# Attention and expert layer on one core: the order of issue planned anew with SyncE's time per DMA, token-place tables made later, nine head pairs transposed on TensorE

## The chip, the core and the metric

The kernel runs on one core of one Trainium2 chip. The metric is device time in microseconds; before the change the median of three runs is 273.97 us.

## What is computed

There are 4 batches, 8 heads, 768 positions and a head dimension of 64. Attention is local and global with a distance bias, in float32 accuracy:

```
scores = q @ k.T / sqrt(64) - slope[h] * dist
keep   = (key < 8) | (0 <= query - key < 96)
a      = softmax(where(keep, scores, -1e9))
x[b]   = concat over heads of a @ v                        # 768 x 512
```

Then, for each batch, the 128 tokens with the highest `x @ w_gate` go through `relu(xe @ w1) @ w2` (512 to 1024 to 512), weighted by a sigmoid of that score and added to their rows.

## The kernel before, in words

**Pairs and fronts.** Two heads make a pair, so there are 16 pairs (`i`, four for each batch) of 6 query tiles (`t`, 128 queries). For a tile, `attend` makes scores on TensorE (L808, read from the transposed `kT` and `qT`), adds the bias and takes the row maximum on VectorE (L824, out `sn`, `nm`), and takes the exponential on ScalarE (L830, out `pr`). The scores of one tile are called a front here. Then the probabilities are transposed and cut into a float16 high and low part. In an `f` tile TensorE transposes (L858, out `pt`), ScalarE writes the high part `ph` and VectorE the low part `pl` (L357, L358). In a `d` tile ScalarE and VectorE cut first (`pn`, L838 and L845) and a transposing DMA from SyncE's queue (L847) writes `pT`. `blend` multiplies with `vs` and `va` into `po` (L886).

**Preparing a pair.** `prep_pair` cuts q and k into float16 high and low parts and transposes them. For a pair below `PEP` TensorE transposes first (L729) and ScalarE and VectorE cut from PSUM (L737, L739). For the others the strings `KM` and `QM` say which engine cuts: the last two letters of a mode name the engine of the high part and of the low part, P for GpSimd (L710, L720), D for VectorE (L714), A for ScalarE; in a three-letter mode the first letter scales the source in place. Then a transposing DMA brings `k16` to `kT` (L762) and `q16` to `qT` (L767). `k16` and `q16` have one buffer each, the loaded `kn`, `qn` and `vn` two. `VM` says the same for v, which needs no transpose but two small copies `va` (L771, L775).

**Setup.** GpSimd makes index patterns (`setup_iotas`), VectorE the mask and the bias of heads 0 and 1 (L602 to L619), GpSimd the bias of the other heads (L623, L625). `setup_moe` makes the tables with which the expert layer finds tokens: `tie`, `places`, `token` and some small ones, on GpSimd (L275 and L630 to L634).

**Expert layer.** `moe_rank` and `moe_chunk` rank the tokens of a finished batch, gather 128 rows and run three products of split float32 operands for each weight (L428, L450). Its pieces are spread over the fronts of the next batch; the last batch's run alone at the end.

**What sets the order.** All this is entered as steps of a `Program`. A step has an engine, a planned duration, what it reads and writes, and a rank. `Program.order` plays the program through: of the steps of an engine that could start within `WINDOW` ns of the earliest one, the one of lowest rank goes next. It knows a TensorE at half speed after little work, and a port that VectorE and GpSimd share (`port=True`). A DMA step holds the planned SyncE for 60 ns. The result is one list; every engine's queue and SyncE's gets its instructions in that order and runs them in order, waiting only for real data and free buffers. `gates[n]` is front n: a step with a gate can't be planned ahead of it. A gate, a rank or a planned duration moves instructions in the queues and puts no wait on the chip. `LG` and `LGE` gate the loads of pairs, `WLG` those of weights, `PACE`, `AUXG` and `MOEP` the expert layer. `ORD0` is the first pair that uses the order `_D1`, which has one `d` tile (t = 4); the pairs before it and the last use `_BASE`, which has none.

```
if name == "SP":
    e["free"] = start + 60
    dma_free = max(dma_free, start + self.DMA_START) + s["dur"]
    end = dma_free + self.DMA_END
```

Of the kernel before, what the change touches and what calls it, by code (L numbers as in the profile page):

```python
# [18 lines left out]
P = 128  # L19
# [3 lines left out]
GMAX = 8  # L23
LBACK = 96
# [19 lines left out]
_D3 = "d4 f0 b0 d1 d5 f2 b2 b1 f3 b4 b5 b3"  # L44

LG = (-13.9, 0.7)
LGE = {1: (-1, 0.4), 2: (0, 0.7)}
PACE = (9.7, 2.7)
PACE2 = (16.83, 1.13)
AUXG = (2, 300, 6)  # L50
AUXG2 = (2.59, 650.35, 4.4)
MOEP = (1.41, 5.1, 16.8, 42.86)
WLR = (33.6, 0.5)
WLG = (6, 0.5)
BG = 1
BG0 = 1
ORD0 = 10
ORDS = [_BASE] + [_D1]
VR = 0
NR = 6  # L60
FR = 1
VR0 = 5
PEP = 8
TLS = 3
WIN_ = 5.94016
VM = 'PD,PD,PD,PD,PD,PD,PPP,APP,APP,PPP,PPP,PPP,DPP,PPP,PPP,PPP'.split(',')
KM = 'PD,PD,PPP,AD,AD,PD,PD,PD,APP,PD,PD,PD,APP,PD,DPP,APP'.split(',')
QM = 'APP,PPP,PD,PD,PD,PD,PD,PD,PD,PD,PD,APP,APP,PD,DPP,AD'.split(',')

# [27 lines left out]
class Program:  # L97
# [14 lines left out]
    def __init__(self):  # L112
        self.steps = []

    def add(self, eng, dur, fn, w=(), r=(), rank=0.0, tail=0, cols=None, port=False):
# [11 lines left out]
        self.steps.append(dict(eng=eng, dur=dur, fn=fn, deps=deps, rank=rank, tail=tail, bufs=bufs,  # L127
                               heavy=cols is not None, port=port or eng == "POOL",
                               cols=dur * 1.9 if cols is None else cols))

    TICK, FULL = 10240 / 3, 3060
# [15 lines left out]
    def order(self):  # L147
# [20 lines left out]
        port = {"DVE": 0.0, "POOL": 0.0}  # L168
        while len(issued) < len(steps):
            best = None  # L170
            for name, e in engines.items():
                pick = None
                for k in e["ready"]:
                    start = max(ready_t[k], e["free"])
# [14 lines left out]
            start, k, name = best  # L189
# [4 lines left out]
                    taken.add(b)  # L194
                    slots[b.ring].remove(min(slots[b.ring]))
            if name == "SP":
                e["free"] = start + 60
                dma_free = max(dma_free, start + self.DMA_START) + s["dur"]
                end = dma_free + self.DMA_END
            else:  # L200
                dur = s["dur"]
                if name == "PE" and self.filler:
                    while start - e["free"] >= self.FILL_MIN:
                        d = self.pe_time(ticks, e["free"], 213, 512)
                        if e["free"] + d > start + self.FILL_OVER:
# [35 lines left out]
def kernel(  # L241
# [15 lines left out]
    NT = S // P  # L257
# [7 lines left out]
    DE = 2 * D + 2  # L265
# [216 lines left out]
    with ExitStack() as fast:  # L482
# [156 lines left out]
        def setup_tie():  # L639
# [4 lines left out]
        a0 = add(-20)  # L644
        a0("SP", 50, lambda: nc.sync.dma_start(
            out=par_i.rearrange("p a w -> p (a w)"), in_=ints.bitcast(I32).partition_broadcast(P)), w=[B_par_i])
        a0("POOL", 1900, setup_iotas, w=[B_set])
        a0("DVE", 70, setup_par, w=[B_par], r=[B_par_i])
        flags_at = len(prog.steps)
        add(40)("DVE", 490, setup_flags, w=[B_flag], r=[B_par])  # L650
        a0("DVE", 700, setup_causal, w=[B_set])
        a0("DVE", 1500, setup_tables, w=[B_set], r=[B_par])
        bias_steps = {}
        for h in range(H):
            bias_steps[h] = len(prog.steps)
            if h in BHD:
                add(6 * (h // 2) - 7)("DVE", 440, lambda h=h: bias_head(h), w=[(B_bias, h)], r=[B_set])
            else:
                add(6 * (h // 2) - 7)("POOL", 1470, lambda h=h: bias_head_pool(h), w=[(B_bias, h)], r=[B_set])
        add(4)("POOL", 1490, setup_moe, w=[B_pos, B_tie, B_pl, B_scol, B_tok, B_filled])  # L660
        add(4)("DVE", 100, setup_tie, w=[B_tie], r=[B_pos])
        add(4)("SP", 300, lambda: nc.sync.dma_start(out=wg_bc, in_=w_gate.partition_broadcast(P)), w=[B_wg])

        def load_weights():
            n = 0
            for src, hi, lo, bh, bl, cols in ((w1, w1_hi, w1_lo, B_w1h, B_w1l, F), (w2, w2_hi, w2_lo, B_w2h, B_w2l, DM)):
                for c in range(src.shape[0] // P):
                    for o in range(0, cols, F32_ROW):
                        sl = slice(o, o + F32_ROW)
# [3 lines left out]
                        a("SP", 730, lambda raw=raw, src=src, c=c, sl=sl: nc.sync.dma_start(  # L673
                            out=raw(), in_=src[c * P:(c + 1) * P, sl]), w=[raw])
# [15 lines left out]
        def prep_pair(i):  # L690
# [103 lines left out]
        def attend(i, t, n, by_dma):  # L794
# [39 lines left out]
            if by_dma:  # L834
# [6 lines left out]
                else:  # L841
# [89 lines left out]
        def finish(a, b, x, t0):  # L931
# [46 lines left out]
        for i in range(NP):  # L978
# [23 lines left out]
            if hp == NPAIR - 1:  # L1002
# [214 lines left out]
```

## Time and profile before

| | us |
|---|---|
| runs, median (lowest, highest) | 273.97 (273.80, 277.82) |
| profiled execution | 275.46 |
| its span, first to last instruction | 273.5 |
| TensorE, VectorE, ScalarE, GpSimd busy | 234.9, 201.6, 204.0, 175.6 |
| mean granted clock of TensorE | 0.917 |

The profiled execution is one run: its own time is 0.5% above the median, and 1.96 us of it lie outside its span. A busy engine is one that has an instruction in it, also one that is held up in it or runs at half clock. No engine is busy all the time, so what sets the end has to be looked for stretch by stretch.

### The profile page before, as it was taken

Reading aid. Unit: us, or ns where it says so; the run is one execution under the profiler, and the core shown is the slowest. Engines: PE = TensorE matmul, PEld = TensorE weight load, DVE = VectorE, ACT = ScalarE, POOL = GpSimd, SP = SyncE. Lnnn points to the kernel's source line nnn. Section 1 sums busy time; section 2 is a strip of 40 time slices with the busy share of each in tenths; the row PEclk is TensorE's granted clock in tenths of the full one; section 3 lists DMA queues with packets and bytes.
Section 4 is the critical chain, followed back from the end, with each engine's and each line's share of the span. In section 5 each row is a group of like instructions: output and inputs, shape, how many; then the busy total and the mean of one; then the engine's idle time right before and its main releaser. Section 6 shows DMA issues by size and latency. Waiting matters only on the chain.

```text
span 273.5 us, 8161 instructions
## 1 busy us (share of the span) xinstructions
PE 234.9 (86%) x2983; PEld 183.1 (67%) x2983; DVE 201.6 (74%) x735; ACT 204.0 (75%) x521; POOL 175.6 (64%) x211
## 2 busy tenths in 40 slices
PE   7598997979888895884999998998978999989990
PEld 3376786867776673763887685766756878767770
DVE  7869999999797788367776689977559688674120
ACT  2348995979889999785799999996799997180200
POOL 9692295997899948869965764899869360111011
PEclk9659997999999999576599999996599999999999
DMA  4999895888999261999978899999933610511011
GB/s 111 234 196 248 198 223 150 214 220 255 311 232 202 62 148 41 167 289 234 225 169 159 143 177 185 202 290 265 153 90 106 131 41 30 203 41 40 2 43 47
DMA packets 114994, 44.28 MB, mean 162 GB/s; under 512 B 107008, under 2 KB 107648, under 8 KB 114944
## 3 DMA queue, kind: packets, MB, share of 16 engines
q1 hardware_dynamic: 114304, 41.57, 70.1%
q0 software_dynamic: 640, 2.10, 2.3%
q8 instruction: 25, 0.41, 0.6%
q14 instruction: 25, 0.20, 0.2%
HBM read 24.38 MB, written 7.34 MB: 116 GB/s over the span
## 4 chain that ended last, share of the span: by engine, by line
PE 41%; DVE 20%; ACT 19%; DMA 8%; issue 5%; POOL 4%; SPq 1%; POOLq 0%; DVEq 0%; ACTq 0%
PE pt L858 7%; PE po L886 6%; PE ps L808 6%; ACT pr L830 5%; DVE pl L358 5%; PE pm L450 5%; PE pm L428 5%; DMA kn<-in_k_dram 5%; DVE sn L824 5%; ACT ph L357 4%; ACT sg L333 3%; PE pm L323 2%; DMA pT<-pn 2%; PE ps L450 2%; PE ps L428 2%
## 5 line engine op out<-in xcount | busy, mean ns | idle before, releaser
L830 ACT ACTIVATE pr<-sn,nm 128x232 f32<-128x232 f32 (+1 forms) x192 | 83.7, 476 | 7.2 <-DVE nm L824 5.8
L824 DVE CUSTOM_DVE_ANT_0 sn<-ps,bias 128x232 f32<-128x232 f32 (+1 forms) x192 | 66.3, 372 | 13.6 <-PE ps L808 11.7
L358 DVE TENSOR_TENSOR pl<-pt,ph 128x512 f16<-128x512 f32 (+1 forms) x91 | 56.9, 635 | 13.7 <-ACT ph L357 13.1
L858 PE MATMUL pt<-ident,pr 128*128 128x128 f32 x332 | 61.0, 310 | 1.3 <-ACT pr L830 1.2
L808 PE MATMUL ps<-kT,qT 64*128 64x128 f16 (+1 forms) x1056 | 50.9, 225 | 8.8 <-DVE nm L824 3.9
L357 ACT CAST ph<-pt 128x512 f16<-128x512 f32 (+1 forms) x91 | 48.7, 545 | 10.3 <-PE pt L858 9.6
L808 PEld LDWEIGHTS <-qT 64*128 64x128 f16 x1056 | 33.4, 99 | 24.2 <-issue 20.6
L858 PEld LDWEIGHTS pt<-ident,pr 128*128 128x128 f32 x332 | 39.6, 154 | 8.3 <-ACT pr L830 4.3
L886 PEld LDWEIGHTS <-ph 128*128 128x128 f16 (+1 forms) x664 | 36.6, 102 | 10.4 <-issue 2.8
L886 PE MATMUL po<-vs,ph 128*128 128x65 f16 x364 | 42.5, 200 | 0.7 <-ACT num L900 0.6
L909 POOL TENSOR_TENSOR x<-num,dens 128x384 f32<-128x384 f32 x30 | 25.4, 845 | 23.0 <-DVE dens L904 12.3
L886 PE MATMUL po<-va,pl 104*128 104x65 f16 x150 | 30.1, 201 | 11.5 <-DVE pl L358 11.2
L886 PE MATMUL po<-va,ph 104*128 104x65 f16 x300 | 37.1, 200 | 1.4 <-ACT ph L357 0.9
L886 PE MATMUL po<-vs,pl 128*128 128x65 f16 x182 | 34.8, 200 | 0.9 <-DVE pl L358 0.9
L886 PEld LDWEIGHTS <-pl 104*128 104x128 f16 (+1 forms) x332 | 23.4, 102 | 14.6 <-DVE pl L358 14.4
L947 POOL TENSOR_TENSOR xw<-x,wg_bc 128x512 f32<-128x512 f32 x18 | 23.4, 1326 | 0.2
L683 POOL TENSOR_TENSOR w_lo<-xw,w_hi 128x512 fp32r<-128x512 f32 x16 | 20.4, 1275 | 0.5
L333 ACT ACTIVATE sg<-sbc,neg 128x768 bf16<-128x768 f32 x21 | 19.6, 935 | 0.1
L710 POOL TENSOR_SCALAR vs<-vn 128x768 f16<-128x768 f32 x16 | 13.5, 846 | 9.6 <-PE po L886 5.6
L456 POOL DMA_INDIRECT out_dram<-xe,idx x4 | 4.1, 1031 | 21.0 <-DVE xe L454 19.8
L720 POOL TENSOR_TENSOR vs<-vn,vs 128x768 f16<-128x768 f32 x10 | 16.2, 1619 | 1.8 <-DVE vn L710 1.6
L900 ACT COPY num<-po 128x390 f32<-128x390 f32 x30 | 14.5, 484 | 3.0 <-PE po L886 2.7
(189 smaller groups left out, 484.2 us busy)
## 6 DMA issues: line engine op xcount, KB each, us to landing
vn<-in_v_dram SPq DMA_DIRECT2D x32, 192.0 KB, 4.4
out_dram<-x SPq DMA_DIRECT2D x24, 256.0 KB, 4.3
kn<-in_k_dram SPq DMA_DIRECT2D x30, 192.0 KB, 4.1
qn<-in_q_dram SPq DMA_DIRECT2D x30, 192.0 KB, 3.8
xw<-in_moe_w_dram SPq DMA_DIRECT2D x16, 256.0 KB, 4.2
va<-vs SPq DMA_DIRECT2D x16, 243.8 KB, 3.7
va<-vs SPq DMA_DIRECT2D x16, 20.3 KB
kn<-in_k_dram SPq DMA_DIRECT2D x2, 128.0 KB
```

Of the source, the lines that this page charges most:

```text
L333: nc.scalar.activation(sg(), flat(), AF.Sign, bias=neg()[:, t:t + 1], accum_out=rank()[:, t:t + 1])
L357: add("ACT", 50 + int(0.836 * cols), lambda: nc.scalar.copy(hi[1](), ps[1]()), w=[(hi[0], part)], r=[ps[0]])
L358: add("DVE", 40 + int(1.04 * cols), lambda: nc.vector.tensor_tensor(out=lo[1](), in0=ps[1](), in1=hi[1](), op=ALU.subtract), w=[(lo[0], pa ...
L428: nc.tensor.matmul(psh(), lhsT=a()[:, d, :], rhs=w[:, d, sl], start=(j == 0), stop=(j == len(mms) - 1))
L683: a("POOL", 1225, lambda raw=raw, hi=hi, lo=lo, c=c, sl=sl: nc.gpsimd.tensor_tensor(out=lo[:, c, sl], in0=raw(), in1=hi[:, c, sl], op=ALU. ...
L808: nc.tensor.matmul(ps[hh]()[:, at:at + n], lhsT=qT()[rows, l, t, :], rhs=kf[rows, r, o:o + n], start=(j == 0), stop=(j == 2))
L824: nc.vector.tensor_tensor_reduce(out=sn()[:, hh, 0:w], in0=ps[hh]()[:, 0:w], in1=bt, scale=-SCALE / QS, scalar=BIG, op0=ALU.add, op1=ALU.m ...
L830: a("ACT", 209 + int(0.836 * w), lambda hh=hh: nc.scalar.activation(pr()[:, hh, 0:w], sn()[:, hh, 0:w], AF.Exp, bias=nm()[:, hh:hh + 1], s ...
L858: nc.tensor.transpose(pt()[:, blk, hh, :], pr()[:, hh, blk * P:(blk + 1) * P], ident)
L886: nc.tensor.matmul(po()[:, g, cols], lhsT=l, rhs=r, start=(m == 0), stop=(m == len(mms) - 1))
L909: a("POOL", 800, lambda: nc.gpsimd.tensor_tensor(out=xv(), in0=num()[:, :, 1:1 + P].rearrange("p t (h d) -> p t h d", h=2), in1=rb(), op=A ...
L947: a("POOL", 1225, lambda t=t, xw=xw: nc.gpsimd.tensor_tensor(out=xw(), in0=x()[:, t - t0, :], in1=wg_bc, op=ALU.mult), w=[xw], r=[x, B_wg] ...
```

## The change

`Program.add` takes `issue`, the time for which a DMA step holds the planned SyncE: 500 ns, or what a line names. `setup_moe` becomes a step of 4700 ns, gated to front 6, the first of pair 1. Pair 8 goes to TensorE's transposes (`PEP` 9). The order with one `d` tile starts at pair 6 (`ORD0` 6), which gives nine `d` tiles (pairs 6 to 14) for five (10 to 14). Planned durations of setup steps, gates, paces and the engines' modes of some pairs get other values.

```
-LGE = {1: (-1, 0.4), 2: (0, 0.7)}
-PACE = (9.7, 2.7)
-PACE2 = (16.83, 1.13)
-AUXG = (2, 300, 6)
-AUXG2 = (2.59, 650.35, 4.4)
-MOEP = (1.41, 5.1, 16.8, 42.86)
+LGE = {1: (-2.5, 0.4), 2: (-1, 0.7)}
+PACE = (10.25, 2.7)
+PACE2 = (15.74, 1.13)
+AUXG = (1.43, 300, 6.37)
+AUXG2 = (3.2, 1143.26, 5.74)
+MOEP = (1.41, 5.07, 17.14, 42.98)
-WLG = (6, 0.5)
-BG = 1
+WLG = (6, 0.3)
+BG = 3
-ORD0 = 10
+ORD0 = 6
-VR = 0
+VR = 1
-VR0 = 5
-PEP = 8
+VR0 = 4
+PEP = 9
-WIN_ = 5.94016
-VM = 'PD,PD,PD,PD,PD,PD,PPP,APP,APP,PPP,PPP,PPP,DPP,PPP,PPP,PPP'.split(',')
-KM = 'PD,PD,PPP,AD,AD,PD,PD,PD,APP,PD,PD,PD,APP,PD,DPP,APP'.split(',')
-QM = 'APP,PPP,PD,PD,PD,PD,PD,PD,PD,PD,PD,APP,APP,PD,DPP,AD'.split(',')
+WIN_ = 22.2261
+VM = 'PD,APP,PD,PD,PD,PD,PPP,PD,PPP,PPP,PPP,DD,DPP,PPP,PPP,PPP'.split(',')
+KM = 'PD,PD,PPP,PD,DPP,PD,PD,PD,APP,PD,PPP,PD,APP,PD,PD,PD'.split(',')
+QM = 'AD,PPP,PD,PD,PD,PPP,PD,DD,PD,PD,PD,APP,PPP,AD,PPP,DPP'.split(',')
+SUM = 6
...
             if name == "SP":
-                e["free"] = start + 60
+                e["free"] = start + s["issue"]
...
-        a0("POOL", 1900, setup_iotas, w=[B_set])
+        a0("POOL", 2000, setup_iotas, w=[B_set])
...
-        a0("DVE", 700, setup_causal, w=[B_set])
-        a0("DVE", 1500, setup_tables, w=[B_set], r=[B_par])
+        a0("DVE", 900, setup_causal, w=[B_set], port=True)
+        a0("DVE", 1700, setup_tables, w=[B_set], r=[B_par], port=True)
...
-        add(4)("POOL", 1490, setup_moe, w=[B_pos, B_tie, B_pl, B_scol, B_tok, B_filled])
+        moe_at = len(prog.steps)
+        add(4)("POOL", 4700, setup_moe, w=[B_pos, B_tie, B_pl, B_scol, B_tok, B_filled])
...
+        prog.steps[moe_at]["deps"].add(gates[SUM])
```

The heads 0 and 1's bias steps get `port=True` as well. The named issue times are 430 ns for weights and outputs, 2500 for `kT`, 1500 for `qT`, 570 and 780 for the two `va`, 1250 for `pT`.

## Rows read from the trace of the kernel before

**Rows 1.** The page, 40 slices of the span: TensorE's granted clock in tenths.
```profile
PEclk9659997999999999576599999996599999999999
```

**Rows 2.** Stretches, us: length, busy us (instructions) of PE, PEld, DVE, ACT, POOL, clock, DMA share, GB/s.
```profile
7.50:10.70 3.20, 0.06 (x4) 0.01 (x1) 3.13 (x11) 0.03 (x1) 1.43 (x2) 0.80 1.10 240
10.70:20.00 9.30, 8.98 (x68) 6.69 (x67) 6.28 (x21) 5.08 (x12) 8.53 (x12) 0.52 1.00 215
24.00:32.00 8.00, 6.93 (x127) 5.60 (x126) 7.71 (x28) 6.67 (x18) 0.39 (x2) 1.00 1.07 232
80.00:96.00 16.00, 13.30 (x223) 10.46 (x217) 12.60 (x51) 15.51 (x43) 16.00 (x16) 1.00 0.70 148
106.00:110.00 4.00, 1.17 (x16) 0.81 (x15) 4.00 (x7) 4.00 (x10) 4.00 (x3) 0.80 0.15 44
114.00:118.00 4.00, 2.20 (x36) 1.67 (x35) 0.83 (x6) 3.31 (x9) 4.00 (x4) 0.85 1.19 267
122.00:126.00 4.00, 1.26 (x23) 1.14 (x22) 2.26 (x3) 0.72 (x2) 3.05 (x3) 0.93 1.21 174
126.00:136.00 10.00, 9.22 (x112) 7.43 (x113) 7.57 (x34) 8.01 (x22) 9.58 (x10) 0.51 1.04 255
184.00:188.00 4.00, 2.30 (x36) 2.18 (x36) 3.30 (x11) 2.13 (x7) 4.00 (x7) 0.86 1.19 274
188.00:197.00 9.00, 9.00 (x70) 7.20 (x68) 5.64 (x22) 7.86 (x23) 7.47 (x7) 0.50 1.05 205
```

**Rows 3.** Timeline of GpSimd, 2 to 10 us: start us, us, instruction, count.
```profile
2.61 0.21 POOL L596 MEMSET vs<- 128x12 f16 x1
...
4.01 2.56 POOL L275 IOTA places<- 128x768 f16 x1
```

**Rows 4.** Timeline of VectorE, 2 to 13 us, same columns, idle time before in brackets.
```profile
2.07 2.20 DVE L602 TENSOR_SCALAR causal<-rel 128x352 f32<-128x352 f32 x1 [0.67 <-POOL rel L275]
4.19 2.54 DVE L604 TENSOR_SCALAR keep<-rel 128x128 f32<-128x128 f32 x1
...
8.32 0.35 DVE L614 TENSOR_SCALAR keep<-keep 128x360 f32<-128x360 f32 x1
...
10.22 0.41 DVE L739 SCALAR_TENSOR_TENSOR kT<-pm,kT 128x256 f16<-128x256 f32 x1
...
12.06 0.28 DVE L824 CUSTOM_DVE_ANT_0 sn<-ps,bias 128x128 f32<-128x128 f32 x1
```

**Rows 5.** Timeline of VectorE, 106 to 127 us: pair 7's last front, pair 8's first, a q part.
```profile
106.29 0.40 DVE L824 CUSTOM_DVE_ANT_0 sn<-ps,bias 128x232 f32<-128x232 f32 x1
...
116.70 0.29 DVE L824 CUSTOM_DVE_ANT_0 sn<-ps,bias 128x128 f32<-128x128 f32 x1 [2.68 <-PE ps L808]
...
123.74 1.57 DVE L714 SCALAR_TENSOR_TENSOR q<-qn,q 128x768 f16<-128x768 f32 x1 [2.26 <-POOL q L710]
```

**Rows 6.** Timeline of SyncE's queue, 111 to 181 us: start us, us of issue, DMA, count.
```profile
111.36 2.98 SPq L762 DMA_TRANSPOSE kT<-k  x1
...
118.58 0.95 SPq L555 DMA_DIRECT2D qn<-in_q_dram  x1
...
180.66 1.34 SPq L847 DMA_TRANSPOSE pT<-pn  x1
```

**Rows 7.** DMA issues by line: count, median us from issue to landing.
```profile
kT<-k SPq DMA_TRANSPOSE x8, 6.0
```

**Rows 8.** Groups by line: operation and shapes, count, busy us, mean ns, idle us before.
```profile
L729 PE MATMUL pm<-ident,qn 128*128 128x128 f32 x48 | 9.0, 300 | 1.1 <-DVE kT L739 1.1
L858 PE MATMUL pt<-ident,pr 128*128 128x128 f32 x332 | 61.0, 310 | 1.3 <-ACT pr L830 1.2
L358 DVE TENSOR_TENSOR pl<-pt,ph 128x512 f16<-128x512 f32 (+1 forms) x91 | 56.9, 635 | 13.7 <-ACT ph L357 13.1
L845 DVE TENSOR_TENSOR pn<-pr,pn 128x464 f16<-128x464 f32 x5 | 5.3, 1052 | 0.0
```

**Rows 9.** Waits, all of the span: us in total, times, longest.
```profile
PEld L886 <- DMA pT<-pn: 1.7, 2, 1.4
```

More of the change, by code (lines that the diff above doesn't have):

```diff
@@ L46 @@
 LG = (-13.9, 0.7)
-LGE = {1: (-1, 0.4), 2: (0, 0.7)}
-PACE = (9.7, 2.7)
-PACE2 = (16.83, 1.13)
-AUXG = (2, 300, 6)
-AUXG2 = (2.59, 650.35, 4.4)
-MOEP = (1.41, 5.1, 16.8, 42.86)
+LGE = {1: (-2.5, 0.4), 2: (-1, 0.7)}
[4 more added lines that the diff above has]
+MOEP = (1.41, 5.07, 17.14, 42.98)
 WLR = (33.6, 0.5)
-WLG = (6, 0.5)
-BG = 1
+WLG = (6, 0.3)
+BG = 3
 BG0 = 1
-ORD0 = 10
+ORD0 = 6
 ORDS = [_BASE] + [_D1]
-VR = 0
+VR = 1
 NR = 6
 FR = 1
-VR0 = 5
-PEP = 8
+VR0 = 4
+PEP = 9
 TLS = 3
-WIN_ = 5.94016
-VM = 'PD,PD,PD,PD,PD,PD,PPP,APP,APP,PPP,PPP,PPP,DPP,PPP,PPP,PPP'.split(',')
-KM = 'PD,PD,PPP,AD,AD,PD,PD,PD,APP,PD,PD,PD,APP,PD,DPP,APP'.split(',')
-QM = 'APP,PPP,PD,PD,PD,PD,PD,PD,PD,PD,PD,APP,APP,PD,DPP,AD'.split(',')
+WIN_ = 22.2261
+VM = 'PD,APP,PD,PD,PD,PD,PPP,PD,PPP,PPP,PPP,DD,DPP,PPP,PPP,PPP'.split(',')
+KM = 'PD,PD,PPP,PD,DPP,PD,PD,PD,APP,PD,PPP,PD,APP,PD,PD,PD'.split(',')
+QM = 'AD,PPP,PD,PD,PD,PPP,PD,DD,PD,PD,PD,APP,PPP,AD,PPP,DPP'.split(',')
+SUM = 6
 class Buf:
@@ L113, in __init__, with add @@
         self.steps = []
-    def add(self, eng, dur, fn, w=(), r=(), rank=0.0, tail=0, cols=None, port=False):
+    def add(self, eng, dur, fn, w=(), r=(), rank=0.0, tail=0, cols=None, port=False, issue=500):
         k = len(self.steps)
@@ L127, in add @@
         self.steps.append(dict(eng=eng, dur=dur, fn=fn, deps=deps, rank=rank, tail=tail, bufs=bufs,
-                               heavy=cols is not None, port=port or eng == "POOL",
+                               heavy=cols is not None, port=port or eng == "POOL", issue=issue,
                                cols=dur * 1.9 if cols is None else cols))
@@ L490, in add @@
         def add(rank):
-            return lambda eng, dur, fn, w=(), r=(), tail=0, drank=0.0, cols=None, port=False: prog.add(
-                eng, dur, fn, w, r, rank + drank, tail, cols, port)
+            return lambda eng, dur, fn, w=(), r=(), tail=0, drank=0.0, cols=None, port=False, issue=500: prog.add(
+                eng, dur, fn, w, r, rank + drank, tail, cols, port, issue)
         def ring(pool, shape, dtype, name, bufs, free=False):
@@ L656 @@
             if h in BHD:
-                add(6 * (h // 2) - 7)("DVE", 440, lambda h=h: bias_head(h), w=[(B_bias, h)], r=[B_set])
+                add(6 * (h // 2) - 7)("DVE", 440, lambda h=h: bias_head(h), w=[(B_bias, h)], r=[B_set], port=True)
             else:
                 add(6 * (h // 2) - 7)("POOL", 1470, lambda h=h: bias_head_pool(h), w=[(B_bias, h)], r=[B_set])
-        add(4)("POOL", 1490, setup_moe, w=[B_pos, B_tie, B_pl, B_scol, B_tok, B_filled])
+        moe_at = len(prog.steps)
+        add(4)("POOL", 4700, setup_moe, w=[B_pos, B_tie, B_pl, B_scol, B_tok, B_filled])
         add(4)("DVE", 100, setup_tie, w=[B_tie], r=[B_pos])
@@ L673, in load_weights @@
                         a("SP", 730, lambda raw=raw, src=src, c=c, sl=sl: nc.sync.dma_start(
-                            out=raw(), in_=src[c * P:(c + 1) * P, sl]), w=[raw])
+                            out=raw(), in_=src[c * P:(c + 1) * P, sl]), w=[raw], issue=430)
                         aux_gate.append((len(prog.steps) - 1, max(0, WLG[0] + WLG[1] * n)))
@@ L763, in prep_pair @@
                 out=kT().rearrange("p s t c -> p (s t) c")[:, :, 0:P], in_=k16().rearrange("p s t d -> p (s t d)")),
-                w=[(kT, "m")], r=[k16])
+                w=[(kT, "m")], r=[k16], issue=2500)
               firsts()
@@ L768, in prep_pair @@
                 out=qT().rearrange("p s t c -> p (s t) c"), in_=q16().rearrange("p s t d -> p (s t d)")),
-                w=[qT], r=[q16])
+                w=[qT], r=[q16], issue=1500)
             parts(vn, lambda s: vs()[:, :, s, 1:1 + P], vs, VM[i % len(VM)], VR if i else VR0)
@@ L772, in prep_pair @@
                 out=va()[0:LBACK].rearrange("p t s d -> p (t s d)"),
-                in_=vs()[P - LBACK:P, 0:NT - 1].rearrange("p t s d -> p (t s d)")), w=[(va, 0)], r=[vs])
+                in_=vs()[P - LBACK:P, 0:NT - 1].rearrange("p t s d -> p (t s d)")), w=[(va, 0)], r=[vs], issue=570)
             gv = "p t s d -> p t (s d)"
@@ L776, in prep_pair @@
                 out=va()[LBACK:BLK_A].rearrange(gv),
-                in_=vs()[0:GMAX, 0:1].rearrange(gv).to_broadcast([GMAX, NT - 1, 2 * DE])), w=[(va, 1)], r=[vs])
+                in_=vs()[0:GMAX, 0:1].rearrange(gv).to_broadcast([GMAX, NT - 1, 2 * DE])), w=[(va, 1)], r=[vs], issue=780)
             ps = pm()
@@ L848, in attend @@
                     out=pT().rearrange("p s h a t -> p (s h a) t"), in_=pn().rearrange("p s h c -> p (s h c)")),
-                    w=[pT], r=[pn])
+                    w=[pT], r=[pn], issue=1250)
                 left = lambda s, hh, blk: pT()[0:BLK_A if blk else P, s, hh, blk, :]
@@ L937, in finish @@
                 a("SP", 730, lambda t=t: nc.sync.dma_start(out=out[b][t * P:(t + 1) * P, :], in_=x()[:, t - t0, :]),
-                  w=[(B_out[b], t)], r=[x])
+                  w=[(B_out[b], t)], r=[x], issue=430)
                 if b == B - 1:
```

## The prediction, made blind

> **What bounds the kernel now.** I read the page first, for the clock. TensorE is granted less than full speed in a few slices only [rows 1], so there are distinct places where it starved. I then cut the span there [rows 2]; what to see is how little TensorE did, and what clock it got afterwards. From 7.5 to 10.7 us it worked 0.06 us, and in the 9.3 us that follow it has a clock of 0.52, which is the lower level (1.2 of 2.4 GHz), and is busy for 8.98. Around 106, 114 and 122 it worked 1.17, 2.20 and 1.26 us of 4 each, and then 9.22 of 10 at 0.51. Around 184 it worked 2.30 of 4, then 9.00 of 9 at 0.50. Each gap thus costs its idle time, and after it about 10 us at half clock.
>
> The first gap is VectorE's. Its two mask instructions last 2.20 and 2.54 us, where one of such a shape takes 0.35 later [rows 4]. The second ends within 0.2 us of GpSimd's `places` pattern, which runs from 4.01 to 6.57 [rows 3]. So VectorE was held up there while GpSimd had its long instruction.
>
> The gaps at 106 and 114 are pair 8's. Pair 7's last front is read at 106.29, pair 8's first at 116.70, after a wait for the scores [rows 5]. They needed `kT`, whose transposing DMA was issued at 111.36 and takes 2.98 us of SyncE to issue [rows 6] and 6.0 to land [rows 7]. Pair 8 is the first that goes by DMA, and GpSimd, which cuts its k, is full from 80 to 96 (16.00 of 16) [rows 2]. The gap at 122 comes from SyncE's order: a q load issued at 118.58 [rows 6] has to land, GpSimd has to cut it, and VectorE stands 2.26 us before the low part of it [rows 5], with low parts and fronts of the running pair queued behind.
>
> **The change, part by part**, against the profiled execution's 275.46 us; I carry the sum over to the median, 1.49 us lower, unchanged.
>
> *Tables out of the setup.* GpSimd is then done with its small patterns and memsets at 2.82 [rows 3]. Held until there at most, the two mask instructions end at 2.82 + 2 x 0.35 = 3.5 in place of 6.73 [rows 4], and the first low part of `kT` comes at 7.0 in place of 10.22. TensorE's gap there is 3.1, so **-3.1** (0, if the first loads then come late, to -3.1).
>
> *The clock behind it.* Without the gap the clock need not fall at 9.4. At most half of the 8.98 busy us would go (-4.5), at least nothing. VectorE is busy 6.28 of the same 9.3 [rows 2], so much of it is paced elsewhere: **-1.5**, a third.
>
> *The tables made later.* They are planned no earlier than front 6, where GpSimd is empty (0.39 busy of 8 from 24 to 32), so GpSimd pays nothing; if that cover is gone they push pair preparation back by their length, which the plan puts at 4.7 us. But VectorE is full there (7.71 of 8). It can be held up as in the setup, by at most 2.20 + 2.54 - 2 x 0.35 = 4.0, at least by nothing: **+1.0**, nearer to nothing, because its work there is mostly subtractions and fronts and not the kind held in rows 4. The Trainium skill (SBUF — State Buffer, SBUF: two separate sides) says that the port pair of VectorE and GpSimd is locked for a whole instruction, and that a VectorE instruction with two SBUF inputs contends only with GpSimd work that reads SBUF. Patterns and memsets read none, so by that this term would be 0 and the sum 1.0 lower; rows 3 and 4 agree for the mask instructions, and no row shows the other kind.
>
> *Pair 8 on TensorE.* 12 transposes of 0.300 us come to TensorE, +3.6 [rows 8]. From GpSimd go two high parts and one subtraction, from SyncE two transposing DMAs. The wait for pair 8's `kT` goes, and its `kn` and `qn` buffers come free sooner, so pair 10's loads can be issued sooner. The three gaps hold 2.83 + 1.80 + 2.74 = 7.4 us of idle TensorE. What is late next is pair 9, now the first by DMA, out of the same full GpSimd. I keep half: **-3.7** (0 to -7.4). The clock behind, from 126: at most half of 9.22, **-1.9** (0 to -4.6).
>
> *Four more `d` tiles* (pairs 6 to 9). TensorE loses 4 x 4 x 0.310 = -5.0 [rows 8]. With pair 8's transposes its work is **-1.4** (+3.6 if only pair 8's addition is on the path, -5.0 if only the saving is). VectorE pays 4 x (1.052 - 0.635) = 1.7 more [rows 8], hidden while TensorE or ScalarE sets the pace; uncovered, it is those 1.7. SyncE issues four `pT` of 1.34 each [rows 6], 5.4, and loses pair 8's two transposes, some 4 to 6 at `kT`'s price. Behind a `pT` that waits for its `pn` stand the next loads, and behind a late `pT` stands `blend` on TensorE. Of the five before, TensorE's weight loads waited twice for a `pT`, 1.4 us at the longest [rows 9]; the costly one is that of 180.66 [rows 6], ahead of the gap at 184. It cost 1.7 idle and at most 4.5 more by the clock. At one in five, four more bring 0.8 of one; at 2.5 each, nearer to what was surely lost, **+2.0** (0 to 4 x 6.2 = 25, the end of the slower rival).
>
> *SyncE's planned time, gates, paces and modes.* These only move instructions in queues. Counted by letters, beside pair 8, GpSimd loses one subtraction and VectorE gets one, of 1.57 us by the one in rows 5, among 15 pairs: **0** (±1.6). What the new SyncE order is worth at the gap of 122 is in the -3.7 already.
>
> Sum: -3.1 - 1.5 + 1.0 - 3.7 - 1.9 - 1.4 + 2.0 = -8.6. That is 266.9 for the profiled execution and **265.4 us** for the median.
>
> **The rivals.**
>
> *The hole only moves.* Pair 9 starves as pair 8 did, or another order of SyncE frees no wait. For it: GpSimd's full stretch of rows 2 stays. Against it: pair 9 loses the wait for the single `k16` and `q16` that pair 8 held. Then the two middle terms are 0: -8.6 + 5.6 = -3.0, **271.0**. The Trainium skill (DMA: Bandwidth & Descriptors, Issuing engines are not separate DMA queues) calls the time to initiate a DMA usually small relative to the DMA itself, by which planning with it would move little and this rival would be the case. Here 2.98 us of issue stand against 6.0 to landing [rows 6, 7], so the trace speaks against the rule for transposing DMAs.
>
> *Slower: `pT` comes late.* Nine transposing `pT` in SyncE's single queue, the new ones at 80 to 130 us where it also loads, stores and transposes. If two more of them land after their `blend` is due, at 6.2 each, SyncE's backlog has eaten the middle gain too: -3.1 - 1.5 + 1.0 - 1.4 + 12.4 = +7.4, **281.4**. With one it is +1.2, so it decides from the second. Against it: the five before made TensorE wait twice, and only once for long [rows 9].
>
> *All of it comes.* Every gap and its slow clock go, the tables cost nothing: -3.1 - 4.5 - 7.4 - 4.6 - 1.4 + 2.0 = -19, **255**.
>
> **How the numbers follow.** The forecast gets 0.50, the moved hole 0.30, late `pT` 0.12, all of it 0.08. The predicted time is the first, 265.4. Its own range, from the ends of the terms that can't all fall together, is 259 to 270. The range to hold 8 in 10 adds the moved hole with 4 us for the tables' upper end and leaves out most of the last two cases: 258 to 275.5. Two per cent, about what a measurement of this kernel can tell from no change, is 268.5 and 279.5. Faster: nearly all of the forecast, the last case and a little of the moved hole, 0.57. Within: 0.32. Slower: 0.11.
>
> **What would show it.** Setup: the mask instructions under 0.9 us each, the first front read near 9 us, and the clock of the second slice full. If they stay near 2 us, or the first front stays at 12, the first two terms are wrong. Tables: VectorE instructions of over 1.5 us beside `places` after pair 1's first front would show the +1.0 or more. Middle: pair 8's first front within 2 us of pair 7's last; if the same 10 us stand before pair 9's, it is the moved hole. `pT`: waits of TensorE in `blend` for the DMA of `pT`, and how many. The prediction is wrong as a whole if the gaps of TensorE come at other pairs and last as long as before, which rows of this trace can't show beforehand.

## The result, and the profile after

| | before | after |
|---|---|---|
| median, us (lowest to highest, runs) | 273.88 (270.2 to 277.82, 4) | **259.0** (255.73 to 263.38, 4) |
| profiled execution; its span | 275.46; 273.5 | 258.79; 256.7 |
| TensorE, VectorE, ScalarE, GpSimd busy | 234.9, 201.6, 204.0, 175.6 | 224.9, 200.0, 201.4, 175.0 |
| mean granted clock | 0.917 | 0.971 |

The change makes the kernel 14.9 us faster: 0.946 of the time before, interval 0.930 to 0.962. Forecast were 8.6, so the time lies 6.4 us below the predicted 265.4.

Look at the clock first, as before. The page's 40 slices of the kernel after:

```profile
PEclk9997999999999999979979999999979999999999
```

Against [rows 1], nothing under 0.7 is left. The mean clock gives the size: at half clock for a share s of the span the mean is 1 - s/2, so 2 x 0.083 x 273.5 = 45 us before and 2 x 0.029 x 256.7 = 15 us after. TensorE's busy time falls by 10.0 us, though only 1.4 of work were to go.

Stretches of the kernel after, columns as in [rows 2] (101 to 105 is where pair 8 starts now):

```profile
7.50:10.70 3.20, 1.72 (x24) 1.09 (x23) 2.43 (x9) 2.35 (x7) 2.20 (x4) 1.00 1.26 228
10.70:20.00 9.30, 7.30 (x104) 5.48 (x104) 7.75 (x34) 8.06 (x21) 8.70 (x13) 1.00 1.05 216
80.00:96.00 16.00, 14.69 (x241) 11.98 (x239) 14.78 (x56) 15.95 (x42) 16.00 (x15) 1.00 0.73 154
101.00:105.00 4.00, 3.38 (x48) 2.79 (x49) 3.34 (x15) 4.00 (x12) 3.97 (x6) 1.00 1.54 172
126.00:136.00 10.00, 8.81 (x66) 6.34 (x67) 8.50 (x23) 7.83 (x19) 5.45 (x4) 0.83 0.99 219
184.00:188.00 4.00, 2.42 (x42) 1.92 (x40) 3.30 (x11) 4.00 (x14) 3.57 (x5) 0.92 1.00 190
188.00:197.00 9.00, 9.00 (x83) 6.59 (x82) 6.09 (x22) 7.99 (x24) 8.15 (x8) 0.85 0.73 114
```

At the start TensorE works 1.72 us where it worked 0.06, and the 9.3 us behind have the full clock: 104 matmuls in 7.30 busy us, where 68 took 8.98. From 80 to 96 GpSimd is as full as before. At 184 the gap is still there (2.42 of 4), but the clock behind it is 0.85, not 0.50.

VectorE's timeline, the instructions of [rows 4] and [rows 5] (start, us, instruction):

```profile
2.08 0.95 DVE L604 TENSOR_SCALAR causal<-rel 128x352 f32<-128x352 f32 x1 [0.68 <-POOL rel L277]
2.95 0.21 DVE L606 TENSOR_SCALAR keep<-rel 128x128 f32<-128x128 f32 x1
...
7.84 0.42 DVE L742 SCALAR_TENSOR_TENSOR kT<-pm,kT 128x256 f16<-128x256 f32 x1 [1.11 <-ACT qT L740]
...
9.63 0.29 DVE L827 CUSTOM_DVE_ANT_0 sn<-ps,bias 128x128 f32<-128x128 f32 x1 [0.44 <-PE ps L811]
...
20.34 0.39 DVE L827 CUSTOM_DVE_ANT_0 sn<-ps,bias 128x232 f32<-128x232 f32 x1
...
22.09 0.69 DVE L742 SCALAR_TENSOR_TENSOR kT<-pm,kT 128x512 f16<-128x512 f32 x1
...
101.77 0.39 DVE L827 CUSTOM_DVE_ANT_0 sn<-ps,bias 128x232 f32<-128x232 f32 x1
...
104.19 0.28 DVE L827 CUSTOM_DVE_ANT_0 sn<-ps,bias 128x128 f32<-128x128 f32 x1
```

The two mask instructions are short, the first front is read at 9.63, and pair 8's first front (104.19) comes 2.4 us after pair 7's last (101.77); it was 10.4. GpSimd makes `places` later, in the kernel after:

```profile
20.00 2.54 POOL L277 IOTA places<- 128x768 f16 x1
...
22.87 1.55 POOL L723 TENSOR_TENSOR vs<-vn,vs 128x768 f16<-128x768 f32 x1
```

Of the waits in the kernel after (total, times, longest), TensorE's for a `pT` are hardly more than in [rows 9], with nine `pT` for five:

```profile
PEld L889 <- DMA pT<-pn: 2.1, 4, 1.2
```

**Where the time came from.** For every kernel below I cut the span at three readings of VectorE (`sn`): the first front of all, pair 7's first, and the last. Times in us, from its timeline:

| kernel | to the first front | to pair 7's first | to the last reading | to the end | median of runs |
|---|---|---|---|---|---|
| before | 12.1 | 83.8 | 134.1 | 43.6 | 273.88 |
| after | 9.6 | 80.1 | 122.1 | 44.8 | 259.0 |
| a1 (before, tables later) | 9.6 | 85.4 | 134.7 | 43.5 | 272.93 |
| a2 (after, tables early) | 12.0 | 80.3 | 122.9 | 46.3 | 261.84 |
| q1 (before, one q load early) | 12.1 | 82.7 | 128.9 | 43.6 | 271.21 |
| r5 (before, pair 8 on TensorE) | 12.1 | 83.1 | 130.1 | 44.5 | 268.76 |
| r3 (after, pair 8 by DMA) | 9.6 | 78.4 | 134.7 | 45.7 | 268.82 |
| r4 (after, five `d` tiles) | 9.4 | 81.7 | 121.5 | 46.9 | 261.99 |
| r2 (before, SyncE's times) | 11.3 | 87.4 | 134.7 | 47.3 | 278.45 |
| r1 (after, SyncE at 60 ns) | 12.5 | 85.3 | 126.7 | 45.5 | 272.1 |
| n1 (after, one planned number) | 9.4 | 80.9 | 127.1 | 47.9 | 266.55 |
| n3 (after, old gates) | 9.0 | 86.2 | 128.4 | 44.5 | 271.11 |
| n2 (after, old modes) | 9.1 | 88.8 | 137.5 | 43.6 | 280.83 |
| s1 (after, r1's SyncE queue) | 8.9 | 99.3 | 137.4 | 44.7 | 293.01 |

By stages the span changes by -2.4, -3.7, -12.0 and +1.2. Of the -12.0, 8.1 come before pair 10's first front (54.1 us from pair 7's first, now 46.1). The stages are of the profiled execution, the medians of all runs. Ratios and intervals leave out the runs that lie over 1.5% above the quickest of their kernel, and the profiled executions of before, a1, a2, r5 and r2 are such runs (1.6, 2.3, 1.8, 2.9 and 4.2 us above the medians), so differences of stages that are no larger are not read. The kernel before ran beside every group of these runs with medians from 273.88 to 274.47, so the medians can be set side by side.

### The profile page after: what moved, and what is told of

The parts are those of the page before. It is cut to its first block, busy times and chain, and to the rows that moved or that the text cites. A ratio compares the mean times of both kernels' runs of the same rounds, so it can differ in the third digit from the quotient of the medians.

```text
span 256.7 us, 8139 instructions
## 1 busy us (share of the span) xinstructions
PE 224.9 (88%) x2979; PEld 173.2 (67%) x2979; DVE 200.0 (78%) x739; ACT 201.4 (78%) x521; POOL 175.0 (68%) x209
## 4 chain that ended last, share of the span: by engine, by line
PE 40%; ACT 16%; DMA 14%; DVE 14%; POOL 6%; issue 5%; SPq 2%; POOLq 0%; DVEq 0%; ACTq 0%
PE pm L430 7%; PE pm L452 5%; PE ps L811 5%; PE pt L861 5%; ACT pr L833 5%; PE po L889 5%; DMA pT<-pn 4%; DVE pl L360 4%; DVE sn L827 4%; ACT sg L335 3%; ACT ph L359 3%; POOL xw L950 3%; DMA kT<-k 3%; DMA kn<-in_k_dram 2%; PE ps L452 2%
## 5 line engine op out<-in xcount | busy, mean ns | idle before, releaser
L360 DVE TENSOR_TENSOR pl<-pt,ph 128x512 f16<-128x512 f32 (+1 forms) x87 | 54.0, 633 | 6.1 <-ACT ph L359 5.7
L861 PE MATMUL pt<-ident,pr 128*128 128x128 f32 x316 | 54.0, 291 | 2.8 <-ACT pr L833 2.3
L811 PE MATMUL ps<-kT,qT 64*128 64x128 f16 (+1 forms) x1056 | 47.4, 217 | 4.7 <-DVE nm L827 2.9
L811 PEld LDWEIGHTS <-qT 64*128 64x128 f16 x1056 | 31.1, 96 | 20.8 <-issue 14.9
L889 PE MATMUL po<-vs,ph 128*128 128x65 f16 x348 | 39.5, 195 | 1.9 <-ACT num L903 1.9
L861 PEld LDWEIGHTS pt<-ident,pr 128*128 128x128 f32 x316 | 35.1, 145 | 8.9 <-ACT pr L833 5.9
L889 PEld LDWEIGHTS <-ph 104*128 104x128 f16 (+1 forms) x632 | 33.6, 99 | 7.9 <-issue 2.8
L889 PE MATMUL po<-va,ph 104*128 104x65 f16 x284 | 34.0, 195 | 0.4 <-ACT ph L359 0.2
L889 PE MATMUL po<-vs,pl 128*128 128x65 f16 x174 | 32.4, 195 | 1.0 <-DVE pl L360 0.6
L889 PEld LDWEIGHTS <-pl 128*128 128x128 f16 (+1 forms) x316 | 21.3, 98 | 8.5 <-DVE pl L360 8.0
L827 DVE DVE_READ_ACCUMULATOR2_ANT nm<- 128x1 f32 x192 | 15.8, 82 | 0.0
```

The costliest lines, as they stand in the source:

```text
L360: add("DVE", 40 + int(1.04 * cols), lambda: nc.vector.tensor_tensor(out=lo[1](), in0=ps[1](), in1=hi[1](), op=ALU.subtract), w=[(lo[0], pa ...
L811: nc.tensor.matmul(ps[hh]()[:, at:at + n], lhsT=qT()[rows, l, t, :], rhs=kf[rows, r, o:o + n], start=(j == 0), stop=(j == 2))
L827: nc.vector.tensor_tensor_reduce(out=sn()[:, hh, 0:w], in0=ps[hh]()[:, 0:w], in1=bt, scale=-SCALE / QS, scalar=BIG, op0=ALU.add, op1=ALU.m ...
L861: nc.tensor.transpose(pt()[:, blk, hh, :], pr()[:, hh, blk * P:(blk + 1) * P], ident)
L889: nc.tensor.matmul(po()[:, g, cols], lhsT=l, rhs=r, start=(m == 0), stop=(m == len(mms) - 1))
```

## Experiments

**Theory at the start:** two holes are closed, the one of the start and pair 8's, with the half clock behind them; the rest of the new list is worth nothing. **Rival:** the holes are a small part, and the gain sits in the list of issue as a whole (SyncE's times, gates, modes).

### The tables: a1 and a2

a1 takes the list of before and moves only the tables behind front 6; a2 takes the list of after and moves them back to the setup.

```diff
a1:  +  return move(o, [moe_at, moe_at + 1], gates[6])
a2:  +  return move(move(o, [moe_at], flags_at - 2), [tie_at], flags_at + 2)
```

> The list of the kernel before, word for word, with the two steps of the token-place tables taken out and put in behind front 6. My theory (the tables held VectorE up in the setup, and the low clock behind it cost as well): the two mask instructions last under 1 us each, the first front is read near 9 us instead of 12, the clock of the second slice is full, and the time falls by 3 to 5 us, to 269 to 271. The rival (the loads of the first pairs set the pace of the start, so that what is gained there is waited for later): the first front comes early, pair 3's first front comes when it did before, and the time is within 1 us of the kernel before.

> The list of the changed kernel, word for word, with the token-place tables put back right behind the setup patterns on GpSimd and their VectorE step behind the mask. My theory: the first front moves from 9.6 to about 12.5 us, the clock falls near 9.4 for some 10 us, and the time rises by 3 to 5 us over the changed kernel, to 262 to 264. The rival: the time stays within 1 us of the changed kernel, because the loads set the pace.

a1: 272.93 us, ratio 0.993 (0.989 to 0.998), 1.9 us faster. a2: 261.84 us, ratio 0.947 (0.938 to 0.955), practically the ratio of after; its runs (258.6 to 263.6) lie among those of after (255.7 to 263.4), so no loss is shown. Both stay short of the 3 to 5 us of my theory. The hole does what it was said to do: with the tables out, a1's first front comes at 9.6, and with them in, a2's at 12.0. But a1 gives much of the 2.5 us back: pair 1 starts 4.7 us sooner and pair 2 only 1.1. The timelines of GpSimd, TensorE and VectorE in a1 say why:

```profile
18.13 2.53 POOL L275 IOTA places<- 128x768 f16 x1
...
21.00 0.84 POOL L711 TENSOR_SCALAR vs<-vn 128x768 f16<-128x768 f32 x1
```

```profile
21.90 0.82 PE L784 MATMUL pm<-vs 128*128 128x128 f16 x6 [2.60 <-POOL vs L711]
```

```profile
19.16 1.66 DVE L640 TENSOR_SCALAR tie<-pos 128x128 bf16<-128x128 f32 x1
```

The tables stand in GpSimd's queue ahead of pair 1's v, and TensorE waits 2.60 us for that v. `tie`, one input from SBUF, is held beside `places` for 1.66 us, where it takes 0.22 in a2's setup; the low part and the front behind it in VectorE's queue (19.39 and 20.00) end with it, at 20.83. The half clock moves too. In the 40 slices of a1 the second and third, low in [rows 1], are full, and the fourth (20.5 to 27.3 us), in which that wait ends, is low:

```profile
PEclk9995997999999999755799999995599999999997
```

In a2 the half clock that was to last some 10 us lasts 3.4, from 12.2. And from its first front a2 reaches pair 7 as fast as after (80.3 to 80.1 us): what the new list gains on that way is not the tables'.

### Pair 8: r5, r3 and the q load of q1

r5 is the kernel before with one number changed, r3 the kernel after with the same number changed back; the planner then makes a new list. q1 is before's own list with one DMA moved: the second half of pair 10's q load is issued right behind the first.

```diff
r5 (before):  -PEP = 8   +PEP = 9
r3 (after):   -PEP = 9   +PEP = 8
q1 (before):  +  return move(o, [load_steps[10][3]], load_steps[10][2])
```

> The kernel before with PEP 9 alone: pair 8 on TensorE, the list planned anew with the old 60 ns. My theory (the hole before pair 8 was the wait for its kT): pair 8's first front follows pair 7's last within 2 to 3 us instead of 10.4, and the time falls by 5 to 10 us, to 264 to 269. The rival (it is the planned time of SyncE that heals the middle): the hole stands before pair 9 instead, and the time is 271 to 274.

> The changed kernel with PEP 8: pair 8 again by transposing DMA. My theory: pair 7's to pair 10's first front takes 52 to 56 us again instead of 46.0, with TensorE waiting before pair 8, and the time rises to 265 to 269. The rival (the plan that knows SyncE's time has pair 8's kT ready): no front later than 3 us after the one before at pair 8, and 258 to 262.

> The list of the kernel before with one DMA moved: the second half of pair 10's q load goes out right behind its first half, some 17 us earlier on SyncE. My theory (SyncE's order alone made the gap of TensorE at 122 to 126): that gap goes, 2.7 us and a part of the low clock behind it, and the time falls by 3 to 5 us, to 269 to 271. The rival (what is late next, the single buffer of the cut q or kT of pair 9, makes the same gap): VectorE or TensorE waits as long within 5 us of it and the time is within 1 us of the kernel before.

r5: 268.76 us, ratio 0.977 (0.970 to 0.984), 6.4 us faster by the ratio. r3: 268.82, ratio 0.977 (0.967 to 0.987), 9.8 us more than after. q1: 271.21, ratio 0.988 (0.980 to 0.997), 3.3 us faster.

VectorE in r5, pair 7's last front and pair 8's first:

```profile
108.35 0.39 DVE L824 CUSTOM_DVE_ANT_0 sn<-ps,bias 128x232 f32<-128x232 f32 x1
...
110.94 0.29 DVE L824 CUSTOM_DVE_ANT_0 sn<-ps,bias 128x128 f32<-128x128 f32 x1
```

and the same two in r3, then SyncE's queue there:

```profile
99.43 0.39 DVE L827 CUSTOM_DVE_ANT_0 sn<-ps,bias 128x232 f32<-128x232 f32 x1
...
108.53 0.28 DVE L827 CUSTOM_DVE_ANT_0 sn<-ps,bias 128x128 f32<-128x128 f32 x1
```

```profile
99.21 1.28 SPq L850 DMA_TRANSPOSE pT<-pn  x1
100.76 1.42 SPq L770 DMA_TRANSPOSE qT<-q  x1
102.27 2.78 SPq L765 DMA_TRANSPOSE kT<-k  x1
```

With pair 8 on TensorE the hole is 2.6 us in the old list; with it by DMA it is 9.1 in the new one, although that list was planned with SyncE's times. So the way of pair 8 alone closes this hole. Three transposing DMAs in a row fill SyncE from 99.2 to 105.1 there, and the scores need the last of them. But it is not SyncE's queue alone that makes `kT` late: when `qT` has been issued, at 102.18, GpSimd has only just cut the low part of k:

```profile
99.83 2.36 POOL L723 TENSOR_TENSOR k<-kn,k 128x768 f16<-128x768 f32 x1
```

From pair 7's first front to pair 10's r5 takes 44.4 us, 9.7 less than before, and from there to the last reading 85.6, 5.7 more. This is not all a hole closed and a gain given back, because work moved over the border: before runs 18 matmuls of the first expert product (L428, 5.22 us) ahead of pair 10, and r5 none. From pair 7's first front to the last r5 gains 4.0. The same goes for r3, which has none there where after has 14: its 49.3 us to pair 10 miss the 52 to 56 of my theory, and to the last front it loses 12.6.

q1's moved load, and the low part of q that stood 2.26 us behind it at 123.74 [rows 5]:

```profile
100.40 1.35 SPq L555 DMA_DIRECT2D qn<-in_q_dram  x2
```

```profile
120.80 1.24 DVE L714 SCALAR_TENSOR_TENSOR q<-qn,q 128x768 f16<-128x768 f32 x1
```

The wait is gone. One DMA at another place in SyncE's queue is worth 3.3 us (0.9 to 5.6 by the interval), half of r5's 6.4.

### Four more `d` tiles, and SyncE's times: r4, r1, r2

```diff
r4 (after):   -ORD0 = 6   +ORD0 = 10
r1 (after):   -e["free"] = start + s["issue"]   +e["free"] = start + 60
r2 (before):  -e["free"] = start + 60   +e["free"] = start + s["issue"]   (and the named issue times)
```

> The changed kernel with ORD0 10: five d tiles, none before pair 10. My theory: TensorE has 16 transposes of 0.3 us more, 5 us of work between 79 and 136 us, where it is busy 0.87 of the time; the time rises by 2 to 4 us, to 261 to 263. The first rival (TensorE's work there is hidden): within 1 us, 258 to 260. The second (the pT transfers of pairs 6 to 9 cost more than they save): 255 to 257.

> The changed kernel planned with the old 60 ns for each DMA on SyncE, all else as changed. The kernel before with PEP 9 alone had the whole gain of the middle (pair 7's to pair 10's first front 44.4 us against 54.1) and lost 5.6 us of it after pair 10 (85.6 to the last front against 80.0). My theory now: the time of SyncE in the plan is what keeps the part from pair 10 on short (76.1 us in the changed kernel), so this kernel keeps the middle (44 to 47 us) and takes 80 to 86 from pair 10 on; 262 to 268 in all. The rival (the other parameters do it, or any new plan): the part from pair 10 on stays under 78 and the time within 2 us of the changed kernel, 257 to 261.

> The kernel before planned with SyncE's time for each DMA, nothing else. My theory: it heals the gap of 122 to 126 as the one moved load did (3.3 us), and not the wait before pair 8; 269 to 272. The rival (SyncE's time in the plan is the main cause): the wait before pair 8 goes too, 260 to 266. A third case: a plan with parameters chosen for 60 ns gets worse, 275 or more.

r4: 261.99 us; it gives no interval, and its runs (258.1 to 263.0) lie among those of after, so what the `d` tiles bring is not shown. r1: 272.1 us, ratio 0.998 (0.993 to 1.002), 13.1 more than after. r2: 278.45 us, ratio 1.020 (1.011 to 1.028), slower than before. So taking SyncE's times out of the new plan loses nearly all of the gain, and putting them alone into the old one, with the old parameters, did not help: the hole before pair 8 is still 7.5 us. Each is one new list, so neither is the worth of the part by itself. r1 keeps the middle short, as expected (43.8 us from pair 7's first front to pair 10's); it loses 2.9 us before the first front and 5.2 on the way to pair 7, which I hadn't expected, and 6.8 behind pair 10, where it also has the matmuls of the first expert product that after runs ahead. VectorE in r1 shows how a list loses it. Its tables are late as in after, and yet its first front is at 12.48:

```profile
7.48 0.42 DVE L742 SCALAR_TENSOR_TENSOR kT<-pm,kT 128x256 f16<-128x256 f32 x1 [2.07 <-ACT qT L740]
7.82 1.73 DVE L621 SCALAR_TENSOR_TENSOR bias<-rel,keep 128x360 bf16<-128x360 f32 x2
...
12.48 0.28 DVE L827 CUSTOM_DVE_ANT_0 sn<-ps,bias 128x128 f32<-128x128 f32 x1
```

VectorE idles 2.07 us with the two `bias` instructions queued behind the `kT` that it waits for. In after they stand ahead of it.

### What a new list is worth by itself: n1, n2, n3

These three bear on whether r1's and r3's losses are those of the parts undone. n1 changes nothing of substance: a latency that the planner takes between engines, by 5 ns. n2 takes back the modes, n3 the gates and paces.

```diff
n1 (after):  -OTHER_LATENCY = 140   +OTHER_LATENCY = 145
n2 (after):  VM, KM, QM as before
n3 (after):  LGE, PACE, PACE2, AUXG, AUXG2, MOEP, WLG, BG, VR, VR0, WIN_ as before
```

> A neutral control: the changed kernel with the planner's latency between engines at 145 ns instead of 140, no part of the change touched, the list planned anew. My theory now (much of the gain is that the parameters were chosen together with this one list, so that any new list loses some of it): 261 to 264, with new gaps of TensorE at other places. The rival (the parts of the change carry the gain, a new list of the same parts is as good): within 1.5 us of the changed kernel, 257.5 to 260.5.

> The changed kernel with the three strings of engine modes (VM, KM, QM) of the kernel before. I had costed them at 0, with ends of 1.6 us, by the sums of the engines. If that holds beside the loss of any new list (3 us): 259 to 264. The rival (which engine cuts which pair decides when a pair is ready, and the strings belong to the list): 268 to 280, with fronts late in the first pairs, where v of pair 1 goes from GpSimd and ScalarE back to VectorE.

> The changed kernel with the gates, paces and ranks of the kernel before (LGE, PACE, PACE2, AUXG, AUXG2, MOEP, WLG, BG, VR, VR0, WIN_), all else as changed. I had costed them at 0. If that holds beside the loss of any new list: 259 to 264. The rival (they place the expert layer's work among the fronts, which is right for one list only): 266 to 273, lost from pair 7 on.

n1: 266.55 us, ratio 0.975 (0.960 to 0.989): **7.5 us more than after for a list of the same parts and parameters**, and more than my theory had. Its four runs (264.6 to 268.1) lie above all four of after; by the two intervals the loss is some 2 to 14 us. n3: 271.11, ratio 0.990 (0.968 to 1.012), 12.1 more, of which 6.1 lie on the way to pair 7 and 6.3 behind it. n2: 280.83, ratio 1.023 (1.002 to 1.044), 21.8 more, slower than before. n1's interval overlaps that of r3 and n3, and ends below those of r1 and n2; so only r1 and n2 are shown to lose more than this one new list.

Two stretches of n1, and the same two of after:

```profile
110.00:115.00 5.00, 3.87 (x47) 2.50 (x44) 3.94 (x18) 4.96 (x14) 5.00 (x5) 0.68 0.99 296
115.00:120.00 5.00, 4.35 (x52) 3.62 (x48) 4.03 (x12) 5.00 (x15) 5.00 (x5) 0.50 1.10 268
```

```profile
110.00:115.00 5.00, 3.58 (x38) 2.29 (x36) 3.57 (x16) 4.90 (x15) 5.00 (x6) 0.73 1.40 298
115.00:120.00 5.00, 4.17 (x69) 3.39 (x69) 3.78 (x15) 4.83 (x14) 4.64 (x5) 0.93 0.93 236
```

Both lists let TensorE idle about as long from 110 to 115, and both lose the clock there. In after it is back soon (0.93, 69 matmuls), in n1 it stays at 0.50 (52 matmuls). That stage is 5.0 us longer in n1, and the one to the end 3.1. VectorE's wait for scores grows from 7.6 us in after to 13.8 in n1 (total, times, longest):

```profile
DVE sn L827 <- PE ps L811: 13.8, 15, 2.5
```

n2 loses in both middle stages (pair 2's first front comes at 37.9 us, in after at 31.8). Its longest wait on the way of the low parts, 3.4 us, was 1.3 in after:

```profile
DVE pl L360 <- ACT ph L359: 16.5, 14, 3.4
```

### The queues against each other: s1

If the gain sat in what the four compute engines do and SyncE's order mattered little, after's engine queues with r1's SyncE queue would run as after. s1 does that. (117 of 197 DMAs then stand at another place; the count in the expectation is off.)

> The four engines' queues of the changed kernel, word for word, with SyncE's queue in the order that the plan with 60 ns gave it (127 to 130 DMAs stand at another place; each engine still runs its own list). That plan as a whole took 272.1 us. My theory (what a plan with SyncE's real time repairs is the engines' queues, which then don't stand before data that can't be there yet; SyncE's own order matters less): 261 to 267. The rival (SyncE's order is what was repaired): 268 to 276, with TensorE's gaps where loads or kT are issued late.

293.01 us, ratio 1.075 (1.061 to 1.089), 34 more than after and 21 more than r1, from which SyncE's queue was taken. My theory fell. s1's waits, of GpSimd and of SyncE's queue:

```profile
POOL vs L713 <- DMA vn<-in_v_dram: 20.3, 6, 8.5
...
POOL k L713 <- DMA kT<-k: 14.4, 2, 7.9
```

```profile
SPq L676 <- ACT xw L952: 7.7, 1, 7.7
```

In after GpSimd's two are 0.8 and 1.4 in total, and SyncE's longest before a weight load (L676) is 1.6. The 7.7 us end at 79.74 with a weight load; v loads stand behind it in SyncE's queue (85.94 and 89.43), and GpSimd waits 8.5 us for v, until 93.59. Later GpSimd waits for a `kT`; the `x` of the running pair stands behind in its queue, ScalarE's `num` waits for `x`, and TensorE, which needs the place that `num` empties, stands 6.85:

```profile
128.50 0.83 POOL L713 TENSOR_SCALAR k<-kn 128x768 f16<-128x768 f32 x1 [6.45 <-DMA kT<-k]
...
131.97 0.81 POOL L912 TENSOR_TENSOR x<-num,dens 128x384 f32<-128x384 f32 x1
```

```profile
132.81 0.48 ACT L903 COPY num<-po 128x390 f32<-128x390 f32 x1 [6.33 <-POOL x L912]
```

```profile
133.35 0.27 PE L889 MATMUL po<-vs,ph 128*128 128x65 f16 x2 [6.85 <-ACT num L903]
```

With the engines' queues that it was planned with, this order of SyncE goes with 272.1 us, with these it takes 293.0: the queues don't fit each other.

## Why the prediction was right in sign and short in size

**Tables out of the setup, -3.1, and the clock, -1.5.** The mechanism is right: both signs that I had named are there (0.95 and 0.21 us, first front at 9.63), and the slice's clock is full. The first front gains 2.4, not 3.1: the first low part of `kT` comes at 7.84, where I had 7.0, after 1.11 us of waiting for ScalarE. What stays of both terms is 1.9 in the old list; in the new one none is shown (a2). In a1 the half clock came back one wait later, so its -1.5 did not stay. "What is late next" was pair 1's v, which I hadn't named.

**Tables later, +1.0.** On VectorE it is 0 in after: beside `places` (20.00 to 22.54) the fronts take 0.39 and a low part 0.69, as elsewhere. In a1 it was not 0, by `tie` (1.66) and by GpSimd's queue, where the tables stood ahead of pair 1's v (2.60). The Trainium skill (SBUF — State Buffer, SBUF: two separate sides) says that who starts first keeps the shared ports for its whole instruction, and that a VectorE instruction outside the two-port modes is kept out only where it has two SBUF inputs and GpSimd's reads SBUF. The trace agrees in both: the fronts and the low part run on beside `places`, and `tie`, once held, ends with it (20.82, and `places` at 20.66). With two SBUF inputs a low part of v in n2 (18.45) ran on beside the memsets of `tie` (18.55 to 19.75), 0.96 us where the shortest in after takes 0.95; the prediction had no row for that, and had left the two-port modes out. That `tie` is in such a mode no run here shows.

**Pair 8 on TensorE, -3.7 and -1.9.** The mechanism is right at its place: the hole before pair 8 goes from 10.4 us to 2.6 in r5 and 2.4 in after. -5.6 is close to r5's 6.4, but r5 is a new list, and n1 shows that a new list can move the time by as much, so the closeness may be luck. That SyncE's order made the gap at 122, as I had read it, q1 bears out. The moved hole, which I had given 0.30, did not come: pair 9's first front is 10.0 us behind pair 8's in after, one pair's work.

**Four more `d` tiles, -1.4 and +2.0.** TensorE's weight loads waited 0.4 us more for `pT` in all. The rest can't be told from a new list (r4).

**Idle time and clock.** The span is 16.8 us shorter: TensorE is busy 10.0 us less and idle 6.8 less (span less busy time: 38.6, then 31.8). The forecast had it busy 4.8 less (-1.5 - 1.9 - 1.4) and idle 3.8 less (-3.1 - 3.7 + 1.0 + 2.0). So the clock was sized too small: if 1.4 of work went, some 8.6 us are the clock's (an estimate), where the two terms had 3.4. The idle time fell by what the gaps alone were given, as if the two new costs had not come, but that it fits is luck in part, for it is not where I had put it. From pair 7's first front to pair 10's, and from there to the last (columns as in [rows 2]), first before:

```profile
95.89:150.04 54.15, 44.79 (x576) 35.91 (x577) 38.13 (x137) 46.06 (x112) 39.80 (x40) 0.81 0.86 180
150.04:229.99 79.95, 73.16 (x1012) 56.47 (x1009) 61.32 (x241) 73.17 (x204) 56.16 (x60) 0.94 0.80 153
```

then after:

```profile
89.76:135.84 46.08, 38.93 (x540) 30.23 (x537) 38.78 (x138) 42.32 (x108) 37.68 (x37) 0.93 1.08 209
135.84:211.85 76.01, 69.47 (x1021) 53.21 (x1021) 61.52 (x240) 71.20 (x200) 57.73 (x62) 0.98 0.93 165
```

In the first TensorE idles 2.2 us less, where I had 3.7, and is busy 5.9 less; in the second it idles about as long (6.8 and 6.5) and the clock rises. 259.0 lies at the lower edge of the forecast's own range, 259 to 270.

**The step that failed** is the zero: gates, paces, modes and SyncE's planned time "only move instructions in queues: 0 (±1.6)". On the chip the queues run in order, and moving is where the time is. Measured: a neutral new list +7.5, old gates +12.1, SyncE at 60 ns +13.1, old modes +21.8, one queue from another list +34; in the old list, one DMA moved -3.3. The first four are lists planned anew, so none is the price of its part. Taken alone the tables give 1.9 and pair 8 gives 6.4, 8.3 if they add up; the other 6.6 of the 14.9 come from neither alone. In the stages it shows as the 3.7 us on the way to pair 7, which a2 has with the tables put back, and as the 3.9 behind pair 10. I had worked out one price for that (letters of the modes, 1.57) and no price for order.

The Trainium skill (DMA: Bandwidth & Descriptors, Issuing engines are not separate DMA queues) calls the time to initiate a DMA usually small relative to the DMA itself. For transposing DMAs the runs disagree, as the rows of before did: 2.78 us for the `kT` in r3 against 5.0 to landing there (the median), and 5.5 of SyncE for three in a row between 99.21 and 105.05.

**What stays open.** Only one neutral list was run, so 7.5 is one draw and not a spread, and none was run of before, beside which r5 and r2 would have to stand. r1 loses 5.6 more than n1, so SyncE's times may help within this list; that they do by themselves no run shows. The shares of the gates, of single modes and of the `d` tiles aren't settled. Nor is it settled which instruction's place makes n1's clock stay low: from 105 to 120 us TensorE's longest wait there is 1.12 us.

## What to carry to other kernels

Where a written-out list orders in-order queues, no parameter of its planner is free: run neutral new lists, better several, beside each test of one part, and call only what lies beyond them an effect. Price a hole of TensorE with the half clock behind it, and read the place (first front to first front) apart from the end, but look what work the two lists have put between the same borders. Undoing one part of a list tuned as a whole tells what the list needs, not what the part brings.

## Not expected of the hardware

- One input from SBUF can be enough to be held beside GpSimd's patterns and memsets: `tie` 1.66 us for 0.22, `causal` 2.20 for 0.95, `keep` 2.54 for 0.21. Not always: a `dens` of 128x6 took its usual 0.15 us beside `places` in r1 (29.44). Instructions that read one input from PSUM ran on beside `places` (0.39, 0.69), unless one that was held stood ahead of them.
- SyncE takes 1.2 to 3.5 us to issue a transposing DMA in after, where the median load of q, k and v takes 0.57. The longest in its queue, beside a load:

```profile
101.49 0.54 SPq L557 DMA_DIRECT2D qn<-in_q_dram  x1
102.13 3.54 SPq L770 DMA_TRANSPOSE qT<-q  x1
```

- TensorE's half clock lasted 10.2 us at three places of before (from 9.4, 125.5 and 186.9 us) and 3.4 us at each of four in after (20.1, 112.3, 129.3, 187.4). The gap at 184 is about as long in both (1.70 and 1.58 us idle of 4), and TensorE was busy for all of the 9 us from 188 on, at a granted clock of 0.50 in the one and 0.85 in the other.
